# Sparse attention into a four-matrix feed-forward, one core: q and k of the local heads of batches 5 to 7 turned by DMA transposes instead of TensorE

## The chip, the core and the metric

The kernel runs on one core of a Trainium2 chip, in one launch. The metric is the device time of one execution in microseconds. Each time given is a median over several runs.

## What is computed

Eight batches, eight heads, 576 tokens, 64 values per head, all in float32. Heads 0 to 3 are *local*: a token sees itself and the 31 before it. Heads 4 to 7 are *strided*: a token sees those earlier tokens whose position is equal to its own modulo 32. What follows is a product of two linear layers and two more layers.

```python
scores = (1/sqrt(64)) * q @ k.transpose(0, 1, 3, 2)
rel = pos[:, None] - pos[None, :]
mask_local   = (rel >= 0) & (rel < 32)
mask_strided = (rel >= 0) & (pos[None, :] % 32 == pos[:, None] % 32)
attn = softmax(where(mask of the head, scores, -1e9))       # heads 0..3 local, 4..7 strided
x = (attn @ v).transpose(0, 2, 1, 3).reshape(8 * 576, 512)
out = ((x @ w1) * (x @ w2)) @ w3 @ w_out                     # w1, w2: 512x1024, w3: 1024x1024, w_out: 1024x512
```

## The kernel before, in words

**Order.** Nothing is written in its final order by hand. The kernel records operations (`plan.op`, L65) with the engines that may run them, a planned cost for each engine, dependencies, buffers taken and given, and a rank. `Plan.order` (L88) then plays them through once with those costs while the program is built, and issues every instruction in the order that comes out. Each engine works its own list strictly in that order, and an instruction that must wait holds up all that stands behind it on its engine. All DMAs, loads, stores and DMA transposes, are issued from one queue, that of SyncE (SP). Loads are taken in the order of the list `_loads` (L25).

**Feed-forward.** w3 and w_out are multiplied into one matrix `w34` at the start (transposes at L613, matmuls at L632). After that there are nine tiles of 512 tokens. Each has eight pairs of groups of four 128x512 matmuls, `a` (L902, against w1) and `b` (L918, against w2), whose product is written to `abt`, and then 32 matmuls `o` (L938) against `w34`. The attention of batch b is laid between the matmuls of tile b-1 by its ranks (`_arank`, L19).

**Attention.** Each batch is worked as four head pairs `hp`: 0 and 1 local, 2 and 3 strided. A local pair is cut into 6 blocks of 96 queries, a strided one into 8 classes of 72. For each pair: scores `S` (L751; for a local pair 12 matmuls of 96 columns with the contraction over the 64 values of a head, two heads on the two halves of the array), exp on ScalarE (L769), a mask product on VectorE (L776), `X` (L788 strided, L798 local; probabilities by values), and the normalisation. A local pair is then turned back by six transposes `U` (L867). `S` needs q and k with the head's 64 values on the partitions, so q and k have to be turned. There are two ways in the kernel:

- **On TensorE.** q and k of four heads are loaded in one go, 128 partitions of 4 tokens (`load_qk`, L490, 512 KB each), which covers 512 of the 576 tokens. The other 64 tokens of all eight heads come with `load_rest` (L506). GpSimd casts them to float16 (L310). Then `T` turns 512 tokens of q and k of one pair with eight 128x128 transposes (`fnT`, L702, matmuls at L707), two copies `E` take them from PSUM to `qT` and `kTL` or `kTS` (L717), and `R` (L652, matmuls at L657) with its copies (L665) puts in the 64 tokens left. Local pairs of all batches and strided pairs of batches 0 to 2 are done so.
- **By DMA transposes.** From batch `LB` = 3 on (`cfg lb`), strided pairs are loaded by `load_qs` (L551) as 72 partitions of 8 tokens (`load_s`, L547), cast on GpSimd into `xs16`, and turned SBUF to SBUF by a DMA transpose issued from SP (L568; its operation is `DTop`, L570). In `qT` and `kTS` the token 8w + c then lies at column 80c + w, and a class of the strided pair reads 72 columns in a row.

`qT` (L334) holds one batch. A transpose or an eviction into pair `hp` of it must wait for `S` of the same pair of the batch before; for the DMA transposes this is L571, where it is `S` of both strided pairs. Seven staging buffers `st` take the loads (L298).

The softmax here doesn't subtract the row's maximum and nothing guards it: scores larger than these inputs give would overflow.

## Time and profile before

| | |
|---|---|
| median of 8 runs | 276.09 us (275.22 to 278.59) |
| the profiled execution | 276.08 us, of which the profile's span is 274.0 us |
| instructions in the span | 6186, of them 2353 matmuls |
| busy: PE, PEld, DVE, ACT, POOL | 96%, 53%, 64%, 59%, 47% |
| granted TensorE clock | 1.00 |
| DMA | 52.56 MB, 192 GB/s on average |

PE is TensorE's matmuls and PEld its weight loads, DVE VectorE, ACT ScalarE, POOL GpSimd, SP the queue of SyncE that issues the DMAs. The matmuls are pipelined: the duration of one in the trace is longer than the distance from its start to that of the next one, and only that distance is time that a matmul costs. For example 128x512 matmuls have 379 ns each and start 216 ns apart. Durations of DMA issues are the time that SP is held by them, not the transfer.

### The profile page before, as it was taken

The page shows a single profiled execution, that of the slowest core. Times are in us where ns is not written, and L with a number is a line of the kernel's source. Part 1 is how long each engine was busy: PE and PEld are TensorE (multiplying, and loading weights), DVE is VectorE, ACT ScalarE, POOL GpSimd, SP SyncE. Part 2 cuts the span into 40 slices and gives each one's busy share as a digit, 9 for nine tenths or more (in the row PEclk, how much of TensorE's full clock was granted, in tenths as well). Part 3 has the DMA queues.
Part 4 walks back from the last instruction along what each step waited for, and adds up shares of the span by engine and source line. Part 5 has one row for each costly group of instructions (what it writes and reads, how often), then busy time and mean ns, then how long its engine had stood idle before and what let it go on. Part 6 is the DMA issues. An engine that isn't in the chain of part 4 may idle for free.

```text
span 274.0 us, 6186 instructions
## 1 busy us (share of the span) xinstructions
PE 263.5 (96%) x2353; PEld 146.0 (53%) x2353; DVE 174.6 (64%) x328; ACT 161.7 (59%) x291; POOL 128.6 (47%) x156
## 2 busy tenths in 40 slices
PE   7787899999999999999999999999999999999995
PEld 2465695746555545555555555555545544444443
DVE  6744466777677767875886788587768763321431
ACT  2871478775668745874687558755765675324321
POOL 6765997789969556586574856530000000000000
PEclk9999999999999999999999999999999999999999
DMA  7999999999999988999999999922141012003004
GB/s 255 346 352 250 321 356 364 305 262 295 321 190 204 225 185 256 279 197 168 330 264 205 229 270 233 201 92 49 28 139 41 0 41 115 0 2 153 0 0 154
DMA packets 64581, 52.56 MB, mean 192 GB/s; under 512 B 34152, under 2 KB 53864, under 8 KB 64552
## 3 DMA queue, kind: packets, MB, share of 16 engines
q1 hardware_dynamic: 64552, 52.18, 72.0%
q8 instruction: 18, 0.29, 0.5%
q14 instruction: 11, 0.09, 0.1%
HBM read 39.45 MB, written 9.44 MB: 178 GB/s over the span
## 4 chain that ended last, share of the span: by engine, by line
PE 88%; DMA 7%; POOL 1%; SPq 1%; issue 0%; DVE 0%; POOLq 0%; DVEq 0%
PE ps_o L938 23%; PE ps_b L918 23%; PE ps_a L902 23%; DMA st<-in_moe_w_dram 5%; PE ps_S L751 4%; PE ps_mm L632 3%; PE ps_X L798 3%; PE ps_T L707 3%; PE ps_X L788 3%; PE ps_U L867 2%; DMA st<-in_k_dram 2%; SPq L313 1%; POOL w3n L310 1%; PE ps_tr L613 1%; PE ps_R L657 1%; POOL v16S L310 0%
## 5 line engine op out<-in xcount | busy, mean ns | idle before, releaser
L918 PE MATMUL ps_b<-xT,w2h 128*128 128x512 f16 x288 | 73.9, 379 | 0.0
L902 PE MATMUL ps_a<-xT,w1h 128*128 128x512 f16 x288 | 73.8, 379 | 0.0
L924 DVE TENSOR_TENSOR abt<-ps_b,asb 128x512 f16<-128x512 f32 x72 | 49.4, 690 | 38.1 <-PE ps_b L918 37.7
L306 ACT COPY asb<-ps_a 128x512 f32<-128x512 f32 x72 | 42.1, 587 | 51.5 <-PE ps_a L902 51.3
L938 PE MATMUL ps_o<-w,abt 128*128 128x512 f16 (+1 forms) x296 | 67.4, 374 | 0.0
L938 PEld LDWEIGHTS <-abt 128*128 128x128 f16 x296 | 26.9, 98 | 27.7
L918 PEld LDWEIGHTS <-w2h 128*128 128x128 f16 x288 | 26.6, 98 | 28.1
L902 PEld LDWEIGHTS <-w1h 128*128 128x128 f16 x288 | 26.7, 98 | 27.7
L769 ACT ACTIVATE ps_S<-ps_S 128x576 f32<-128x576 f32 (+2 forms) x56 | 32.8, 626 | 10.5 <-PE ps_S L751 9.9
L306 ACT COPY osb<-ps_o 128x512 f32<-128x512 f32 x35 | 20.6, 588 | 20.6 <-PE ps_o L938 20.3
L310 POOL CAST v16L<-st 32x768 f16<-32x768 f32 (+1 forms) x32 | 26.3, 822 | 7.6 <-DMA st<-in_v_dram 4.6
L854 DVE TENSOR_TENSOR xT<-ps_X,rcp 64x288 f16<-64x288 f32 x56 | 25.1, 449 | 5.9 <-ACT rcp L838 5.3
L310 POOL CAST x<-st 128x1024 f16<-128x1024 f32 x22 | 22.7, 1040 | 12.2 <-DMA st<-in_q_dram 6.8
L776 DVE TENSOR_TENSOR ptm<-ps_S,maskL 128x576 f16<-128x576 f32 x28 | 19.8, 750 | 12.1 <-ACT ps_S L769 12.1
L310 POOL CAST v16S<-st 72x1024 f16<-72x1024 f32 (+1 forms) x16 | 16.5, 1037 | 13.8 <-DMA st<-in_v_dram 12.5
L310 POOL CAST xs<-st 80x1024 f16<-80x1024 f32 x20 | 20.2, 1036 | 4.7 <-DMA qT<-xs 2.6
L817 DVE TENSOR_TENSOR xqs<-ps_X,rcq 96x384 f16<-96x384 f32 (+1 forms) x36 | 20.5, 568 | 1.2
L838 ACT ACTIVATE rcp<-ps_X 64x576 f32<-64x576 f32 x28 | 18.1, 647 | 0.9
L827 ACT ACTIVATE ps_X<-ps_X 64x576 f32<-64x576 f32 x28 | 17.7, 631 | 0.9 <-PE ps_X L788 0.5
L632 PE MATMUL ps_mm<-woh,w3T 128*128 128x256 f16 x128 | 15.9, 272 | 1.6 <-POOL woh L310 1.5
L798 PEld LDWEIGHTS <-ptm 128*96 128x96 f16 (+1 forms) x224 | 14.5, 123 | 5.3
L308 DVE COPY qT<-ps_T 128x512 f16<-128x512 f16 x16 | 11.1, 692 | 7.9 <-PE ps_T L707 7.9
(81 smaller groups left out, 274.8 us busy)
## 6 DMA issues: line engine op xcount, KB each, us to landing
out_dram<-osb SPq DMA_DIRECT2D x35, 256.0 KB
st<-in_moe_w_dram SPq DMA_DIRECT2D x16, 512.0 KB
st<-in_v_dram SPq DMA_DIRECT2D x26, 288.0 KB
st<-in_q_dram SPq DMA_DIRECT2D x11, 512.0 KB
st<-in_k_dram SPq DMA_DIRECT2D x11, 512.0 KB
st<-in_q_dram SPq DMA_DIRECT2D x10, 288.0 KB
st<-in_k_dram SPq DMA_DIRECT2D x10, 288.0 KB
st<-in_moe_w_out_dram SPq DMA_DIRECT2D x4, 512.0 KB
```

What stands on the lines that cost most here:

```text
L306: pin(nc.scalar.copy(out=out, in_=in_))
L310: pin(nc.gpsimd.tensor_copy(out=out, in_=in_))
L632: pin(nc.tensor.matmul(ps, big[f"w3T{kc // 4}"][:, kc % 4, js], big["woh"][:, kc, ns], start=(kc == 0), stop=(kc == KF - 1)))
L769: pin(nc.scalar.activation(out=sps, in_=sps, func=AF.Exp, bias=0.0, scale=scale))
L776: pin(nc.vector.tensor_mul(ptm[0:kr, 0:576].rearrange("p (h a x) -> p h a x", h=2, x=w), pte[0:kr].rearrange("p h (a x) -> p h a x", x=w), ...
L798: pin(nc.tensor.matmul(xps[0:w, h, i * 65:(i + 1) * 65], ptms[pslot][0:kr, c0:c0 + w], vt[0:kr, 2 * (hp % 2) + h, g * m + i, 0:D + 1], sta ...
L817: pin(nc.vector.tensor_mul(xqs[0:w, 0:m].rearrange("p i h d -> p h i d"), xv[:, :, :, 0:D], _ap(rcp, 0, [[rcp.ap[0][0], w], [4, 2], [1, m] ...
L854: pin(nc.vector.tensor_mul(o, i0, i1))
L902: pin(nc.tensor.matmul(ps, w1h[:, ci, js], xT[ci][:, tok], start=(ci == 0), stop=(ci == KM - 1)))
L918: pin(nc.tensor.matmul(ps, w2h[:, ci, js], xT[ci][:, tok], start=(ci == 0), stop=(ci == KM - 1)))
L924: pin(nc.vector.tensor_mul(big[("abt", t)][:, jc, :], bank("f", f"b{t}_{jc}"), live[("asb", t, jc)]))
L938: pin(nc.tensor.matmul(ps, big[("abt", t)][:, ci, bass.ds(ts * P, P)], w34[:, ci, bass.ds(pt * nw, nw)], start=(ci == 0), stop=(ci == KF - ...
```

## The change

A new setting `ll=5` sends the local pairs of batches 5 to 7 through `load_qs` too. For these, `load_qk` and `load_rest` are not called, and `T`, `E`, `R` and its copies are not made (16 transposes and 8 matmuls of `R` in each of the three batches). Instead, for each local pair:

- q is loaded, cast and turned like a strided pair's: 72 rows of 8 tokens, column 80c + w for token 8w + c. A block of 96 queries is then 12 values of w by 8 of c, and `S` reads it as its moving operand with a step of 80 elements (160 bytes) between neighbouring columns.
- k is loaded in rows of single tokens (96 partitions, 12 runs of 256 bytes each, the form in which `load_vL` loads v), cast, and turned so that its tokens lie in `kTL` in their own order.

Two DMA transposes are added per local pair, 12 in all. Other parts of the diff touch all batches: `load_s` now issues two DMAs, for 64 and for 8 rows, where it issued one for 72; a DMA transpose of a pair waits for `S` of that pair of the batch before and no longer for both; the planned costs of SP and of several transfers are changed, so that the order that comes out differs in places. The settings `ub` and `nxq` are added and left at values that use none of their code.

```diff
-        r += [("qk", b, 0), ("r", b), ("vL", b, 0), ("vL", b, 1)]
-        r += [("qk", b, 1)] if b < 3 else [("qs", b, 0), ("qs", b, 1)]
+        r += [("qk", b, 0), ("r", b)] if b < 5 else [("qs", b, 0), ("qs", b, 1)]
+        r += [("vL", b, 0), ("vL", b, 1)]
+        r += [("qk", b, 1)] if b < 3 else [("qs", b, 2), ("qs", b, 3)]
...
-           first=('DVE', 'ACT', 'POOL'), early=0, pm=4, nx=4, nstg=7, new=(2, 3), lb=3)
+           first=('DVE', 'ACT', 'POOL'), early=0, pm=4, nx=4, nstg=7, new=(2, 3), lb=3, ll=5)
...
-        o = plan.op(name, {"SP": 450}, fn, take=[("stg", key)] if first else [], dma=ns)
+        o = plan.op(name, {"SP": 700 if name[:2] == "vL" else 500}, fn, take=[("stg", key)] if first else [], dma=ns)
...
-    def load_s(key, ten, b, hh):
-        src = ten[b, 4 + 2 * hh:6 + 2 * hh].rearrange("h (p c) d -> p h (c d)", c=ST)
-        return dma(key, key, 830, [P, 2, ST, D], lambda s: s[0:SQ].rearrange("p h c d -> p h (c d)"), src, clean=2)
+    def load_s(key, ten, b, hp):
+        src = ten[b, 2 * hp:2 * hp + 2].rearrange("h (p c) d -> p h (c d)", c=ST)
+        return [dma(key, key, 700, [P, 2, ST, D], lambda s: s[0:64].rearrange("p h c d -> p h (c d)"), src[0:64],
+                    clean=2),
+                dma(f"{key}b", key, 100, None, lambda s: s[64:SQ].rearrange("p h c d -> p h (c d)"), src[64:SQ],
+                    first=False)]
...
+            nat = local and nm == "k"
+            if nat:
+                ds = [dma(key, key, 1950, [P, 2, LT, D], lambda s: s[0:LQ].rearrange("p h t d -> p (h t) d"),
+                          _ap(k, (b * H + 2 * hp) * S * D, [[D, LQ], [LQ * D, 2 * LT], [1, D]]))]
+            else:
+                ds = load_s(key, ten, b, hp)
+            nr, nt = (LQ, LT) if nat else (SC, ST)
...
-                o = (qT[:, hp] if nm == "q" else kTS[:, hh, 0:ST * SC]).rearrange("x (c w) -> x c w", w=SC)
+                if nm == "q":
+                    o = qT[:, hp].rearrange("x (c w) -> x c w", w=SC)
+                elif local:
+                    o = kTL[:, hh, 32:32 + S].rearrange("x (c w) -> x c w", w=LQ)
+                else:
+                    o = kTS[:, hh, 0:ST * SC].rearrange("x (c w) -> x c w", w=SC)
...
-            late.append((o, lambda: [Sop.get((b - 1, h)) for h in (2, 3)]))
+            late.append((o, lambda: [Sop.get((b - 1, hp))]))
...
-        for i, nm in enumerate("qk"):
+        for i, nm in enumerate("qk" if b < LL else ""):
...
-            dt = b >= LB and not local
+            dt = b >= (LL if local else LB)
...
-                            pin(nc.tensor.matmul(sps[:, h, i * w:(i + 1) * w], kT[r_, ks:ks + P],
-                                                 qT[r_, hp, qs:qs + w], start=not pm, stop=not pm or i == m - 1))
+                            qq = qT[r_, hp, qs:qs + w]
+                            if dt and local:
+                                q0 = (g * m + i) * LQ // ST
+                                qq = qT[:, hp].rearrange("x (c w) -> x w c", w=SC)[r_, q0:q0 + LQ // ST]
+                            pin(nc.tensor.matmul(sps[:, h, i * w:(i + 1) * w], kT[r_, ks:ks + P], qq, start=not pm, stop=not pm or i == m - 1))
```

## The prediction

> **What bounds the kernel.** I read the page's busy rows and slices first, then its chain of waits. The columns of the second fence are the 40 slices of 6.85 us.

> ```profile
> span 274.0 us, 6186 instructions
> PE 263.5 (96%) x2353; PEld 146.0 (53%) x2353; DVE 174.6 (64%) x328; ACT 161.7 (59%) x291; POOL 128.6 (47%) x156
> ```
> ```profile
> PE   7787899999999999999999999999999999999995
> PEclk9999999999999999999999999999999999999999
> DMA  7999999999999988999999999922141012003004
> ```
> ```profile
> PE 88%; DMA 7%; POOL 1%; SPq 1%; issue 0%; DVE 0%; POOLq 0%; DVEq 0%
> ```

> PE is idle for 274.0 - 263.5 = 10.5 us, in the first five slices, where the chain runs over DMA loads of weights. From there on it is full at a granted clock of 1.00, and 88% of the chain lies on it. The list of what PE waited for, asked for 40 to 272 us alone, comes back empty. So each PE microsecond removed after 40 us is a microsecond off the end, as long as nothing becomes late. DMA is full as well until slice 26 (about 180 us) and then nearly idle; it feeds PE and does not yet hold it up.

> A busy PE is not PE at its peak, so I take prices from starts in the timeline of PE (start, duration, line):

> ```profile
> 195.40 0.43 PE L751 MATMUL ps_S<-qT,kTS 64*128 64x72 f16 x16
> 195.76 1.04 PE L938 MATMUL ps_o<-w,abt 128*128 128x512 f16 x4
> 196.64 0.40 PE L657 MATMUL ps_R<-idR,x16r 96*128 96x64 f16 x8
> 196.87 1.03 PE L938 MATMUL ps_o<-w,abt 128*128 128x512 f16 x4
> 197.74 0.42 PE L788 MATMUL ps_X<-ptm,v16S 72*128 72x72 f16 x8
> 198.00 0.61 PE L707 MATMUL ps_T<-id,x 128*128 128x128 f16 x8
> 198.45 0.42 PE L788 MATMUL ps_X<-ptm,v16S 72*128 72x72 f16 x8
> ```

> One `T` holds PE from 198.00 to 198.45, 0.45 us; one `R` from 196.64 to 196.87, 0.23 us. No idle time stands between the groups.

> **Removed from PE.** Two `T` and one `R` for each of batches 5, 6 and 7: 3 x (2 x 0.45 + 0.23) = 3.39 us, all of it on the path. The order built from the changed kernel has 72 matmuls fewer on PE, just these. Their 12 evictions `E` and 6 of `R` lie on ACT and DVE, 59% and 64% busy and on no percent of the chain: worth nothing.

> **Added on PE: a moving operand with a step.** `S` of a local pair has 12 matmuls of 96 columns, in 6 couples that run side by side on the halves of the array (starts in the trace 3 ns apart within a couple, 40 to 43 ns from one couple to the next: the 216 ns of 512 columns scaled to 96 give 40). Two pairs in three batches make 36 couples, 36 x 40 = 1.46 us of reading. Now each column of q lies 160 bytes from the last. No PE instruction before reads its moving operand so. The nearest row is a DVE copy of 128x576 float16, packed from local pairs and with a step of 8 elements from strided ones (it reads PSUM, `S` reads SBUF):

> ```profile
> L308 DVE COPY xT<-ps_U x17: 456/458/758, 18.5 to 214.8; 128x576 f16<-128x576 f16 x17
> ```

> The packed ones have 458 ns, the two with a step 756 and 758: 1.66 times. On ACT no such loss shows: 639 ns for 576 packed, 586 to 591 for 512 with a step of 4. Lower end: no loss, 0 us (there are no fewer columns to read, so no gain). Upper end: PE reads with a step no faster than that DVE row, 758/576 = 1.32 ns an element, 126 ns a couple instead of 40: 36 x 86 = 3.1 us. I take the ratio 1.66, since the row is of the same kind, two-byte elements with a step: 1.46 x 0.66 = 0.97 us.

> [...]

> **Added on SP, DMA and GpSimd, off the path if they keep up.** SP issues all DMAs in order. Its rows, in two pieces of its timeline:

> ```profile
> 64.83 2.88 SPq L313 DMA_DIRECT2D st<-in_v_dram  x4
> ...
> 77.77 0.34 SPq L313 DMA_DIRECT2D st<-in_k_dram  x1
> ```
> ```profile
> L568 SPq DMA_TRANSPOSE kTS<-xs x10: 1206/1272/2012, 95.0 to 197.6; - x10
> ```

> The first line is v of batch 2 for two strided pairs, as 64 and 8 rows each: 1.44 us per couple of DMAs. One of 72 rows has 0.34. So each strided load costs SP about 1.1 us more. Per batch from 5 on SP issues 8 such couples (11.5 us), 2 loads of k and 2 of v in rows of 256 bytes (about 0.6 each where not held up, 2.4), 8 transposes (8 x 1.27 = 10.2) and 4.5 stores (0.4 each, 1.8): 25.9 us. A batch on PE takes 26.3 us now (its first local `S` starts at 176.80 for batch 6, 203.12 for batch 7) and would take about 25.5. For batches 3 and 4 it is 6 couples, 6 packed loads and 4 transposes, about 19 us. From 75 us, where loads of batch 3 start, that makes 2 x 19 + 3 x 25.9 = 116 us of issuing, done at 191 us if SP never waits. The last transpose is needed for the last `S`, at 221.3 now and near 218.9 then, and lands 2.7 us after its issue starts (188.16 to 190.81 in the trace's completion marks): 25 us are left for waits. The first transposes of batch 7 can start when `S` of the same pair of batch 6 is through (176.8, 182.1) and are needed near 200.5. What is queued behind a waiting transpose on SP is loads of the next batch and stores; stores have three buffers on ACT's side, loads a lead of ten and more us. That cover is why I cost the 12 transposes and the split at nothing; if it is gone, the lateness goes straight to the end, since PE waits in order.

> DMA: by the completion marks, 72-row loads of 288 KB in a row land 1.6 to 1.7 us apart (81.03 to 91.09 us), two 64-row loads of 256 KB 0.6 us apart (69.58, 70.21). The split therefore saves some 0.8 us of DMA on 30 loads, about 24 us. Against it stand, for each of three batches, about 1.6 for q, 2 x 1.2 for k in rows of 256 bytes (loads of v in that form land 0.8 to 1.7 us apart) and 4 x 0.65 for transposes (175.59, 176.17, 176.91, 177.62), 6.6 in all, instead of 4.9 for the two 512 KB loads and the rest: +5 us. DMA has more room than before.

> GpSimd: two casts of 1.04 us and two of 0.61 go, two of 1.04 and two of about 0.82 come: +0.4 us a batch on an engine that is 47% busy. Nothing. The new planned costs shift PE's order between about 27 and 60 us and the strided `S` of batch 7 by one group. The work is the same; the bound is the longest single wait of PE there so far, 1.8 us for `w3n`, either way, and I take 0.

> **The sum.** Profiled execution 276.08 (span 274.0 and 2.1 around it; the median of the runs is 276.09) - 3.39 + 0.97 = 273.7 us. From the bounds of the step alone: 272.7 to 275.8. A measurement here can tell about 0.5% from no change, 1.4 us; the limits are 274.7 and 277.5.

> **Rivals.** (1) *SP becomes the clock.* In 62.5 to 200 us SP is held by its DMA issues for 94.8 us, and some 35 us of these are issues that take far longer than the same issue at its shortest (a transpose 6.2 us instead of 1.2). If these 35 us stay on top of 116 us, SP ends at 75 + 116 + 35 = 226, 10 us after the last transpose is needed, and PE stands still for them: 272.7 + 1 + 10, about 284. It decides once held-up issues and waits pass 25 us. For it: SP's sum is as long as a PE batch. Against: the long issues come where DMA is behind, and the split takes 24 us from DMA. Chance 0.16. (2) *The step costs PE two to three times the contiguous read or more*, up to the 3.1 us above: 274.7 to 276.5. For it: a step of 160 bytes is far wider than the 16 bytes of the DVE row. Chance 0.14. (3) *The freed PE time comes back as another wait*, for `ps` banks or the ACT evictions of `a`: 275 to 276. ACT waited 51.3 us for `a` and is not late, so 0.05. The forecast's own case, a step at up to 2.4 times and no late load, holds 0.65 and 272.4 to 274.7.

> **How the numbers follow.** Faster comes from the forecast's case and a little of (2): 0.67. Within 0.5%: most of (2), (3) and a mild form of (1): 0.18. Slower: the rest of (1): 0.15. The range goes from 272.4 (no loss by the step, 0.3 for the shifted order) to 276.4, which takes in (2), (3) and leaves the full (1) out, with a little beyond each end.

> **What would show it.** Right: 72 matmuls fewer, no `T` or `R` after batch 4, PE's list of waits after 40 us still empty, batches 5 to 7 shorter by 0.8 us each, and `S` of local pairs at 0.53 us from start to next group instead of 0.37. Each step can be wrong by itself: the step, if that distance is 0.37 or above 0.7; SP, if PE's weight loads of `S` wait on `qT` or `kTL`; the queue, if the last transposes land after 215 us. The forecast falls if PE shows more than a microsecond of idle time after 60 us.

## The result, and the profile after

The changed kernel takes 277.63 us (median of 11 runs, 277.31 to 279.23), the kernel before 275.78 us beside it (32 runs): the ratio is 1.0074, 95% interval 1.0055 to 1.0093. It is slower, by about 2 us, where 273.7 us and a gain of 2.4 us were forecast. The profiled execution took 277.48 us, 275.7 of them in the span: 1.7 us more span than before.

The page of the changed kernel, its first rows:

```profile
span 275.7 us, 6098 instructions
PE 266.2 (97%) x2281; PEld 144.7 (52%) x2281; DVE 170.7 (62%) x324; ACT 158.0 (57%) x277; POOL 130.6 (47%) x156
```

PE runs 72 matmuls fewer than before, just those that the forecast took off, and yet is busy for 2.7 us more. The slices, and the chain by engine and by line:

```profile
PE   8887999999999999999999999999999999999995
PEclk9999999999999999999999999999999999999999
DMA  6999999999799998799799986789969003003004
...
PE 87%; DMA 7%; SPq 2%; POOL 1%; issue 1%; ACT 1%; DVE 1%; POOLq 0%; DVEq 0%
PE ps_o L974 23%; PE ps_b L954 22%; PE ps_a L938 22%; DMA st<-in_moe_w_dram 7%; PE ps_S L776 6%; PE ps_mm L650 3%; PE ps_X L822 3%; PE ps_X L812 2%; PE ps_U L903 2%; PE ps_T L727 2%; SPq L314 2%; POOL w3n L311 1%; PE ps_tr L631 1%; PE ps_S L763 0%; PE ps_R L675 0%
```

PE is full after the first slices at the full clock, as before, and asked for 40 to 275 us the list of what PE waited for is empty again. So no wait came in: the added time is inside PE's own work. Of PE's lines on the chain one has grown, `S` (L776, L751 before): 6%, where it was 4%. Its groups, kept apart by shape, before (first line) and after:

```profile
L751 PE MATMUL ps_S<-qT,kTL 64*128 64x96 f16 x192 | 6.9, 204 | 0.0
```
```profile
L776 PE MATMUL ps_S<-qT,kTL 64*128 64x96 f16 x192 | 12.0, 264 | 0.0
```

The columns are busy us, mean ns of one, idle time before. As many matmuls of the local pairs, of one shape, are busy for 5.1 us more. All of it lies in batches 5 to 7. One local `S` group of batch 5 in the timeline of PE, before and then after; what counts is the distance from its start to that of the next group:

```profile
150.47 0.43 PE L751 MATMUL ps_S<-qT,kTL 64*128 64x96 f16 x12
150.83 1.04 PE L938 MATMUL ps_o<-w,abt 128*128 128x512 f16 x4
```
```profile
149.24 1.29 PE L776 MATMUL ps_S<-qT,kTL 64*128 64x96 f16 x12
150.46 1.04 PE L974 MATMUL ps_o<-w,abt 128*128 128x512 f16 x4
```

0.36 us became 1.22 us (0.362 and 1.220 by the trace's nanoseconds), the same in all six groups. Within a group the two matmuls of a couple still start 3 ns apart; the couples start 163 ns (the first two) to 190 ns apart, 183 ns on average, where before they started 53 ns (the first two) and 42 to 43 ns apart. The account closes: 6 x (1.220 - 0.362) = 5.15 us added, 3.41 us of `T` and `R` removed (0.451 and 0.235 a group), +1.74 us, and the span grew by 1.7.

### The profile page after: what moved, and what is told of

Read it like the earlier page. It is cut to its first block, busy times and chain, and to the rows that moved or that the text cites. A ratio compares the mean times of both kernels' runs of the same rounds, so it can differ in the third digit from the quotient of the medians.

```text
span 275.7 us, 6098 instructions
## 1 busy us (share of the span) xinstructions
PE 266.2 (97%) x2281; PEld 144.7 (52%) x2281; DVE 170.7 (62%) x324; ACT 158.0 (57%) x277; POOL 130.6 (47%) x156
## 4 chain that ended last, share of the span: by engine, by line
PE 87%; DMA 7%; SPq 2%; POOL 1%; issue 1%; ACT 1%; DVE 1%; POOLq 0%; DVEq 0%
PE ps_o L974 23%; PE ps_b L954 22%; PE ps_a L938 22%; DMA st<-in_moe_w_dram 7%; PE ps_S L776 6%; PE ps_mm L650 3%; PE ps_X L822 3%; PE ps_X L812 2%; PE ps_U L903 2%; PE ps_T L727 2%; SPq L314 2%; POOL w3n L311 1%; PE ps_tr L631 1%; PE ps_S L763 0%; PE ps_R L675 0%
## 5 line engine op out<-in xcount | busy, mean ns | idle before, releaser
L938 PE MATMUL ps_a<-xT,w1h 128*128 128x512 f16 x288 | 73.8, 379 | 0.0
L311 POOL CAST xs<-st 80x1024 f16<-80x1024 f32 (+1 forms) x32 | 31.7, 997 | 32.6 <-DMA st<-in_k_dram 19.2
L938 PEld LDWEIGHTS <-w1h 128*128 128x128 f16 x288 | 26.6, 98 | 27.6
L311 POOL CAST v16L<-st 32x768 f16<-32x768 f32 (+1 forms) x32 | 26.3, 822 | 9.1 <-DMA st<-in_v_dram 7.7
L311 POOL CAST x<-st 128x1024 f16<-128x1024 f32 x16 | 16.5, 1040 | 11.2 <-DMA st<-in_k_dram 6.9
L309 DVE COPY xT<-ps_U 128x576 f16<-128x576 f16 x17 | 8.4, 493 | 12.5 <-PE ps_U L903 12.5
```

Source lines behind the costliest of these rows:

```text
L311: pin(nc.gpsimd.tensor_copy(out=out, in_=in_))
L938: pin(nc.tensor.matmul(ps, w1h[:, ci, js], xT[ci][:, tok], start=(ci == 0), stop=(ci == KM - 1)))
```

## Experiments

All are edits of the changed kernel. A *group* is the 12 matmuls of `S` of one local pair, and its time is the distance from its start to that of the next group on PE. Times of the kernel before are from the same chip as the runs beside them. Loads, casts and DMA transposes stay as the change has them unless the edit says otherwise.

### e1: q of local pairs in single tokens, so that `S` reads columns in a row

```diff
-            nat = local and nm == "k"
+            nat = local
...
-                           _ap(k, (b * H + 2 * hp) * S * D, [[D, LQ], [LQ * D, 2 * LT], [1, D]]))]
+                           _ap(ten, (b * H + 2 * hp) * S * D, [[D, LQ], [LQ * D, 2 * LT], [1, D]]))]
...
-                if nm == "q":
+                if nm == "q" and local:
+                    o = qT[:, hp, 0:S].rearrange("x (c w) -> x c w", w=LQ)
+                elif nm == "q":
...
-                            if dt and local:
-                                q0 = (g * m + i) * LQ // ST
-                                qq = qT[:, hp].rearrange("x (c w) -> x w c", w=SC)[r_, q0:q0 + LQ // ST]
```

> The changed kernel, but q of the local pairs of batches 5 to 7 is loaded in rows of single tokens like k and lies in qT in its own order, so that S reads 96 columns in a row; all else, the 12 DMA transposes too, stays. Theory A (the step of 160 bytes in the moving operand is the loss: the trace of the changed kernel shows a local S group at 1.22 us to the next group instead of 0.36): these groups go back to 0.36 us, PE loses 6 x 0.86 = 5.15 us, and the span is about 275.7 - 5.15 = 270.6 us, some 1.2% below the kernel before. Rival B (the loss comes from what feeds S: the transposed k in kTL, the fuller SP queue, later landings): the groups stay near 1.2 us and the time within 0.5% of the changed kernel, 276 to 279 us. Rival C (q in rows of 256 bytes makes DMA late): S groups at 0.36 us but PE waits between groups, 272 to 276 us.

280.47 us (278.76 to 280.55) against 275.88; ratio 1.0147, interval 1.0115 to 1.018. The local `S` groups are back at 0.361 us, so the stepped read made them long. But the time rose. PE's waits from 57 us on, and the slices, of this run:

```profile
PE ps_S L775 <- DVE xT L882: 1.7, 2, 0.9
PE ps_a L937 <- DVE xT L882: 1.2, 1, 1.2
PE ps_X L811 <- DVE ptm L799: 1.1, 2, 0.7
...
PE   7787999999999999999999999999999958999995
PEclk9999999999999999999999999999999995999999
```

At 224 to 231 us PE stands five times, for the attention of batch 7 alone: the DVE steps of one pair's attention no longer lie beside other PE work. From the third stop on its clock is down (the 5 at 229 to 236 us) and the 128x512 matmuls start 0.42 to 0.43 us apart instead of 0.216. Added up by starts the stops make about 5 us and the slow clock about 2, a little more than the 277.1 - 270.6 = 6.5 us of span above the expectation. This is the trace of an execution of 278.77 us; four of the six took 280.45 to 280.55, and no trace shows what these 1.7 us more are. No transpose was late: the last `kTS` landed at 215.95, and the `S` that follows on it ran at 225.26. Its place in PE's order was late. This kernel plans its q loads of local pairs at 1950 ns where the change has 700 and 100, so the planner put `S` of batch 7's pairs later. That is a reading; e1b tests it.

### e2: the rest of the change alone

```diff
-        r += [("qk", b, 0), ("r", b)] if b < 5 else [("qs", b, 0), ("qs", b, 1)]
+        r += [("qk", b, 0), ("r", b)] if b < 8 else [("qs", b, 0), ("qs", b, 1)]
...
-           first=('DVE', 'ACT', 'POOL'), early=0, pm=4, nx=4, nstg=7, new=(2, 3), lb=3, ll=5)
+           first=('DVE', 'ACT', 'POOL'), early=0, pm=4, nx=4, nstg=7, new=(2, 3), lb=3, ll=8)
```

> The changed kernel with ll=8: no local pair is turned by DMA, T and R are as before in all batches. What is left of the change is the split of the 72-row loads into 64 and 8 rows, the transposes' wait for one S instead of two, and the new planned costs with the order that comes of them. Theory A: this rest is worth nothing to PE, ratio to the kernel before 0.997 to 1.003. Rival B (the rest is a part of the loss): slower by 0.5% or more. If the rest is a gain hidden by the step: faster by 0.5% or more.

276.23 us (275.34 to 278.88) against 275.88; ratio 1.0012, interval 0.9989 to 1.0035. Split loads, planned costs and the looser wait together are worth nothing that can be told: no loss, and no gain either. The loss is that of the local pairs.

### e3: six steps in one run

Each of the six local `S` groups reads as many columns as before, 96, with another step. They are other columns than the scores need, so the output is not that of the reference.

```diff
-                                qq = qT[:, hp].rearrange("x (c w) -> x w c", w=SC)[r_, q0:q0 + LQ // ST]
+                                st_ = (2, 4, 8, 16, 32, 64)[2 * (b - LL) + hp]
+                                qb = qT[r_, hp, 0:ST * SC]
+                                qq = _ap(qb, q0, [[qb.ap[0][0], 64], [1, 12], [st_, 8]])
```

> The changed kernel, where each local pair of batches 5, 6 and 7 reads q with another step, so that S reads wrong columns of q there (the scores of these pairs are not the reference's); as before 12 groups of 8 columns. Steps in order of the pairs: 2, 4, 8, 16, 32, 64 elements of 2 bytes. Theory A1 (a new 16-byte piece of SBUF at each column is what costs): steps 2 and 4 near 0.36 us for a group of 12 matmuls, steps 8 to 64 all at about 1.2 us. Theory A2 (any step but 1 costs the same): all six at about 1.2 us. Theory A3 (the loss grows with the distance): a rise from step to step, 64 highest.

There is one execution, with a span of 273.8 us, and one group for each step; in the change all six groups took the same 1.22 us, so a difference between groups here is one of the step. The timeline of PE for steps of 2, 4, 8, 32 and 64 elements, each group and the start of the next:

```profile
149.15 0.47 PE L778 MATMUL ps_S<-qT,kTL 64*128 64x96 f16 x12
149.55 0.82 PE L976 MATMUL ps_o<-w,abt 128*128 128x512 f16 x3
...
154.49 0.75 PE L778 MATMUL ps_S<-qT,kTL 64*128 64x96 f16 x12
155.17 0.30 PE L905 MATMUL ps_U<-id,xqs 96*128 96x96 f16 x3
...
174.70 1.17 PE L778 MATMUL ps_S<-qT,kTL 64*128 64x96 f16 x12
175.80 0.39 PE L976 MATMUL ps_o<-w,abt 128*128 128x512 f16 x1
...
201.42 1.14 PE L778 MATMUL ps_S<-qT,kTL 64*128 64x96 f16 x12
202.49 0.39 PE L976 MATMUL ps_o<-w,abt 128*128 128x512 f16 x1
...
207.43 1.14 PE L778 MATMUL ps_S<-qT,kTL 64*128 64x96 f16 x12
208.51 0.39 PE L905 MATMUL ps_U<-id,xqs 96*128 96x96 f16 x5
```

0.40, 0.68, 1.10, 1.08 and 1.08 us (and 1.14 for 16). The price grows up to a step of 8 elements, 16 bytes, and not beyond; the change's own 80 elements cost a little more, 1.22. That a step of 4 would be near 0.36 was wrong: it already costs 0.32 us more.

With a step of 4, most 16-byte pieces of `qT` give two columns in a row, and the group takes 0.68 us all the same: two columns to a piece did not bring PE back to 0.36.

### e4: runs of neighbouring columns

The six groups read runs of 2, of 4, of 8 and of 12 columns, then a mixture in which the upper half of the array steps by 80 elements and the lower reads in a row, then 96 in a row. Again they are other columns than the scores need.

```diff
+                                off, pat = ((0, [[2, 6], [80, 8], [1, 2]]), (0, [[4, 3], [80, 8], [1, 4]]),
+                                            (0, [[40, 12], [1, 8]]), (q0, [[80, 8], [1, 12]]),
+                                            (q0, [[1, 12], [80, 8]] if h == 0 else [[1, 96]]),
+                                            (q0, [[1, 96]]))[2 * (b - LL) + hp]
+                                qq = _ap(qb, off, [[qb.ap[0][0], 64], *pat])
```

> The changed kernel, where each local pair of batches 5 to 7 reads q in another pattern of 96 columns (the scores of these pairs are not the reference's): runs of 2 columns in a row, each run 160 bytes from the last; runs of 4; runs of 8, 80 bytes apart, at 16-byte boundaries; runs of 12, 160 bytes apart; a step of 160 bytes in the upper half of each couple and 96 in a row in the lower half; and 96 in a row in both. If the cost goes by jumps (Theory A1), with about 1.5 us of extra time per 1000 jumps as in the changed kernel (147 ns for a couple's 96): runs of 2 give a group of 0.36 + 0.43 = 0.8 us, of 4 about 0.57, of 8 and 12 about 0.43 to 0.46, or none if a run hides its jump. The half-and-half pattern gives 1.2 us if the halves wait for each other, and the last one 0.36 us. Rival B (k or the DMA feeding): all near 1.2 us.

One execution. The timeline of PE for runs of 2, of 4 and of 8, and for the mixture:

```profile
150.89 0.73 PE L781 MATMUL ps_S<-qT,kTL 64*128 64x96 f16 x12
151.55 0.39 PE L979 MATMUL ps_o<-w,abt 128*128 128x512 f16 x1
...
156.49 0.46 PE L781 MATMUL ps_S<-qT,kTL 64*128 64x96 f16 x12
156.88 0.43 PE L908 MATMUL ps_U<-id,xqs 96*128 96x96 f16 x6
...
176.42 0.43 PE L781 MATMUL ps_S<-qT,kTL 64*128 64x96 f16 x12
176.78 1.04 PE L979 MATMUL ps_o<-w,abt 128*128 128x512 f16 x4
...
201.61 1.28 PE L781 MATMUL ps_S<-qT,kTL 64*128 64x96 f16 x12
202.83 0.39 PE L979 MATMUL ps_o<-w,abt 128*128 128x512 f16 x1
```

0.66, 0.39, 0.36 us, 0.36 for runs of 12, 1.22 for the mixture and 0.36 for 96 in a row. A fixed price for each jump had called for 0.8, 0.57 and 0.43 to 0.46, so that is not the rule. Jumps cost nothing here once eight columns follow on each other (80 bytes from run to run) or twelve (160 bytes), 0.36 us as for 96 in a row. With one half stepping the group takes as long as with both, 1.22 us: the slower half set its time.

### e5: the change with runs of 12

For one and the same data in `qT`, `S` reads c outside and w inside: 8 runs of 12 columns. The queries of a block then come in another order, which a permuted mask and the copy from `U` to `xT` put right (which then reads with a step: 0.76 us on DVE instead of 0.46, and planned at 760 ns instead of 450).

```diff
-                                qq = qT[:, hp].rearrange("x (c w) -> x w c", w=SC)[r_, q0:q0 + LQ // ST]
+                                qq = qT[:, hp].rearrange("x (c w) -> x c w", w=SC)[r_, :, q0:q0 + LQ // ST]
...
-            kr, mk = (P, maskL) if local else (SQ, maskK) if dt else (KB, maskS)
+            kr, mk = (P, maskP if dt else maskL) if local else (SQ, maskK) if dt else (KB, maskS)
...
+                if local and dt:
+                    copy(e, o.rearrange("x (t w c) -> x t w c", w=LQ // ST, c=ST),
+                         ps[:, 0:S].rearrange("x (t c w) -> x t w c", w=LQ // ST, c=ST))
```

> The changed kernel, loads and DMA transposes untouched, but S of the local pairs of batches 5 to 7 reads its 96 columns as 8 runs of 12 in a row instead of one column at each 160-byte step; the queries of a block then stand in another order, so these pairs get a permuted mask, and the copy from U to xT puts the order right again (VectorE 0.30 us more for each of 6 copies, beside the path). Theory A (the jumps at each column are the whole loss): the S groups at 0.36 us as in the run with runs of 12, span 275.7 - 5.15 = 270.6 us, ratio to the kernel before 0.985 to 0.991. Rival (with PE faster, the transposes from SP become late, as the last one landed 10 us before its S in the changed kernel): idle time on PE near 215 to 230 us, 273 to 277 us.

274.87 us (273.5 to 276.66) against 275.93; ratio 0.9953, interval 0.9929 to 0.9978: faster than before, with the loads and transposes of the change as they were, but short of the expected 0.985 to 0.991. The span, 272.3, is 1.7 above what was expected, and PE's waits from 57 us on show most of it:

```profile
PE ps_S L780 <- DVE xT L887: 0.8, 1, 0.8
PE ps_a L945 <- DVE xT L887: 0.4, 1, 0.4
```

`S` of batch 7's first pair stands at 200.72 us, half through, for `xT` of the attention before it; both `kTL` of the batch had landed by 196.44. So it is not a transfer. In e1b, below, 16 matmuls `o` stand between the last `X` before this `S` and the `S`, here 8, and the normalisation has less time: it reads as the planned order again, but no run tests that here.

### e1b: e1 with its loads planned short

```diff
-                ds = [dma(key, key, 1950, [P, 2, LT, D], lambda s: s[0:LQ].rearrange("p h t d -> p (h t) d"),
+                ds = [dma(key, key, 1200, [P, 2, LT, D], lambda s: s[0:LQ].rearrange("p h t d -> p (h t) d"),
```

(on top of e1, so it counts for q and k of these pairs; the number is used by the planner alone)

> The run with q in rows of single tokens again, but with 1200 instead of 1950 as the planned DMA cost of such a load. In that run S was back at 0.36 us and yet the time was longer, since the planned order set attention of batch 7 behind most of tile 6, and its last normalisation stood bare before tile 7. With the shorter cost the order that comes out sets S of batch 7 at the places that it has in the kernel before. If only the planned order was at fault: about 272 to 273 us, ratio 0.985 to 0.992. If the loads or transposes of batch 7 are late in fact: PE waits at S of batch 6 or 7, 274 to 281 us.

272.14 us (272.07 to 272.45) against 275.93; ratio 0.9854, interval 0.982 to 0.9889. This is the best of all the versions. From its page:

```profile
span 270.6 us, 6088 instructions
PE 260.4 (96%) x2281; PEld 142.4 (53%) x2281; DVE 170.7 (63%) x324; ACT 157.6 (58%) x277; POOL 129.2 (48%) x156
```

The span is 274.0 - 3.4 = 270.6: all of `T` and `R` gained, nothing given back. The list of waits from 57 us on is empty, the local `S` groups take 0.361 us, and the last `kTS` lands at 207.40, 10.6 us ahead of the `S` that needs it (218.02; the pair before it has its `S` at 210.72, with `kTS` since 206.15). `S` of batch 7's pairs start at 199.87 to 218.02, 5 to 8 us earlier than in e1. One planned number made the difference between e1 and e1b: 6.5 us between the two profiled spans, 8.3 us between the medians.

### e5 and e1b with another first batch

```diff
-           first=('DVE', 'ACT', 'POOL'), early=0, pm=4, nx=4, nstg=7, new=(2, 3), lb=3, ll=5)
+           first=('DVE', 'ACT', 'POOL'), early=0, pm=4, nx=4, nstg=7, new=(2, 3), lb=3, ll=6)
```

> Runs of 12 as in its neighbour, but for batches 6 and 7 alone (ll=6): two thirds of the removed T and R, 2.27 us instead of 3.41. Theory A: 1.1 us slower than the one from batch 5, ratio to the kernel before 0.989 to 0.995. If SP holds up the one from batch 5, this one is the faster of the two.

> Runs of 12 for batches 4 to 7 (ll=4): T and R of four batches gone, 4.55 us. The planned order sets attention of batch 7 behind most of tile 6, as in the run with q in rows. If PE alone counts: 1.1 us faster than from batch 5, ratio 0.981 to 0.987. If SP is the clock at four batches with 20 DMAs and 8 transposes each: the end of batch 7 stands bare, slower than from batch 5 by 2 us or more.

> Edit: e1b (q of local pairs in rows of single tokens, its load planned at 1200) with the change from batch 4 on instead of batch 5. If PE alone counts: 1.13 us less than e1b (two T of 0.45, one R of 0.23), span 269.5, 271.0 us, ratio to the kernel before 0.981 to 0.983. Rival: with a fourth batch through SP and the DMA transposes the attention of batch 7 is set or fed late, as in the runs-of-12 version from batch 4: idle PE at 200 to 232 us and 274 us or more. It decides whether batch 5 was the right place to begin.

e5 from batch 6: 274.7 us, ratio 0.9941 (0.992 to 0.9962), the same as from batch 5 within the intervals; one batch less to gain from, and fewer stops. e5 from batch 4: 281.43 us, ratio 1.0182 (1.0144 to 1.0219). e1b from batch 4: 276.63 us, ratio 1.0019 (0.9995 to 1.0042), 4.5 us more than from batch 5, where PE's work alone would have given 1.1 less. PE's waits from 57 us on in e5 from batch 4:

```profile
PE ps_a L945 <- DVE xT L887: 4.4, 3, 2.2
PE ps_X L816 <- DVE ptm L804: 1.8, 2, 1.5
```

Again the attention of batch 7 comes late and its DVE steps lie bare (in e1b from batch 4 from 225 to 230 us; the granted clock of that execution is 0.987 on the mean of its span, where e1b has 1.00), though the last `kTS` had landed at 216.65 and 217.64 and the last `S` ran at 226.81 and 224.37. What of this is the planned order and what a late transpose of an earlier pair was not separated.

### e6: is it the run, or the 16 bytes?

Steps of 2 cost as much as runs of 4 (0.40 and 0.39 us), steps of 4 as much as runs of 2 (0.68 and 0.66). That fits a price for each 16-byte block that PE goes on to. The first three of the six patterns here move the runs off the blocks; the others go between two places, go round four, and step by 6. Again they are other columns than the scores need.

```diff
+                                off, pat = ((4, [[40, 12], [1, 8]]), (6, [[16, 3], [80, 8], [1, 4]]),
+                                            (7, [[8, 6], [80, 8], [1, 2]]), (0, [[1, 48], [80, 2]]),
+                                            (0, [[1, 24], [80, 4]]),
+                                            (0, [[1, 12], [6, 8]]))[2 * (b - LL) + hp]
```

> Edit: as e4, with six other reading patterns of q in the six local S groups of batches 5 to 7; these groups read the wrong columns, 96 as ever. In order: runs of 8 that begin at element 4 of a block of 8 (a block is 16 bytes); runs of 4 that begin at element 6; runs of 2 that begin at element 7; columns alternating between two places 80 elements apart; columns going round four places 80 elements apart; step 6. Theory L (what counts is how often PE has to go on to another 16-byte block, about 1.45 to 1.95 ns each by the groups measured so far, with the contiguous 40 ns a couple as floor): the patterns change block 24, 48, 96, 96, 96 and 74 times, so the groups take 0.36 to 0.40, 0.66 to 0.68, 1.08 to 1.22, 1.08 to 1.22, 1.08 to 1.22 and about 0.85 to 0.95 us. Rival R (the length of the run counts, wherever it lies): 0.36, 0.39, 0.66 as measured for aligned runs of 8, 4 and 2, and 1.08 to 1.22 for the other three. Rival H (several blocks are held, so that coming back to one is free): the fourth and fifth at 0.36 to 0.40. Span near 270.6 plus what the six groups take above 0.362 each.

One execution. The timeline of PE for the second, third and fourth pattern (runs of 4 and of 2 across a block's edge, two places in turn):

```profile
155.48 0.74 PE L781 MATMUL ps_S<-qT,kTL 64*128 64x96 f16 x12
156.15 0.43 PE L908 MATMUL ps_U<-id,xqs 96*128 96x96 f16 x6
...
175.68 1.28 PE L781 MATMUL ps_S<-qT,kTL 64*128 64x96 f16 x12
176.90 0.39 PE L979 MATMUL ps_o<-w,abt 128*128 128x512 f16 x1
...
181.83 0.72 PE L781 MATMUL ps_S<-qT,kTL 64*128 64x96 f16 x12
182.49 0.30 PE L908 MATMUL ps_U<-id,xqs 96*128 96x96 f16 x3
```

Runs of 4 take 0.67 us when they straddle an edge and 0.39 when they do not; runs of 2 take 1.21 and 0.66. The length of the run does not explain that, the number of blocks does (48 and 24, 96 and 48). The first, fifth and sixth pattern fit too (0.365, 1.083 and 0.904 us). The fourth does not: two places in turn take 0.655 us, where a new block at each column should give 1.08 or more; four places in turn (1.083) are at the full price. So going back to the block of two columns before cost less than going on to a new one, and going back to that of four columns before cost as much; why stays open.

## Why the prediction was wrong, step by step

**What bounds the kernel** held: PE is full after 57 us before and after, at the full clock, and where no wait came in PE's time moved the end one for one (after +1.74 for +1.7 of span, e1b -3.4 for -3.4).

**The removal from PE** held: 3.39 forecast, 3.41 by the starts, 72 matmuls, and e1b shows it whole at the end.

**The step that failed is the price of the moving operand with a step**: 0.97 us taken, 3.1 us as the upper end, 5.15 us measured. 0.858 us a group is 143 ns a couple, from 40 to 183, 4.6 times; 27 were taken and 86 were the bound. The prediction's sign that a distance above 0.7 us would show this step wrong came out at 1.22. Three errors lie in it. The ratio 1.66 came from a DVE copy, whose contiguous read is itself slow (458 ns for 576 elements, 0.8 ns each); PE starts from 0.42 ns a column, so even the same loss for each element, 0.52 ns, would have been a ratio of 2.2. The bound took for granted that PE reads with a step no slower than DVE; nothing in the trace of before said so. PE took 183 / 96 = 1.91 ns a column, DVE 1.32 ns an element. And the rows were misread: in the kernel before, that copy (L880) reads PSUM with a step of 72 elements, 144 bytes, not 8, and ACT's copy (L721) with one of 128, not 4. ACT showed no loss and DVE 1.66 at steps nearly as wide as the 160 bytes of `S` or wider; the two engines differed, which was a reason to trust neither for PE. With 5.15 in the forecast's own sum, 276.08 - 3.39 + 5.15 = 277.84, against 277.48 in the profiled execution.

**SP, DMA and GpSimd at nothing** held for this change: e2 and e1b show it, and no transpose was late. The last two `kTL` and the last `kTS` in the timeline of SP, after:

```profile
191.99 1.22 SPq L586 DMA_TRANSPOSE kTL<-xs  x1
...
194.62 1.31 SPq L586 DMA_TRANSPOSE kTL<-xs  x1
...
210.89 1.24 SPq L586 DMA_TRANSPOSE kTS<-xs  x1
```

They land at 196.29, 197.47 and 214.28, and their `S` start at 203.07, 209.22 and 224.66. The bound of 215 us was kept by a hair: the 191 us of issuing without waits became 212, so 21 of the 25 us kept for waits were used.

The estimate of DMA behind this term was wrong all the same. It had 24 us saved by the split and 5 us added, "more room than before". The time that the packets of the DMA queue took (packets, MB, share of 16 engines' span), before, with the rest of the change alone (e2), and after:

```profile
q1 hardware_dynamic: 64552, 52.18, 72.0%
```
```profile
q1 hardware_dynamic: 64912, 52.18, 70.1%
```
```profile
q1 hardware_dynamic: 76576, 53.66, 78.1%
```

Of spans of 274.0, 274.7 and 275.7 us that is 197, 193 and 215 us: the split took off some 5 us, and the local pairs' loads and transposes put on some 23 beyond what they replace. DMA got fuller by 18 us instead of emptier by 19, and it cost nothing only because PE waited for none of it.

**The shifted order at 0** held here and is the weakest point beyond: e1 lost 6.5 us of span to the planner's order, and e5 1.7, which is read the same way. **Rival 2** named the right mechanism and capped it too low, at 3.1 us. Its reason, that 160 bytes are far wider than the DVE row's 16, does not stand: that row's step is 144 bytes, and e3 has PE at almost the whole price from 16 bytes on. **Rival 1** did not happen. What resembles it, the versions from batch 4, stood for late attention, and there a late transpose of an earlier pair was not ruled out.

## What to carry to other kernels

In these groups of 96 columns of float16, runs of 8 and of 12 columns cost what 96 in a row cost (0.36 us), runs of 4 took 0.39 us within 16-byte blocks and 0.67 across their edges, runs of 2 took 0.66 and 1.21, and steps of 8 elements and more 1.08 to 1.22. So count the blocks that a matmul's pattern goes through, and choose the layout of the load or the transpose so that the matmul reads in a row (e1b), or reorder the loops of the pattern (e5), before giving up the cheaper path. An upper bound taken from another engine is no bound (1.32 ns an element on DVE, 1.91 ns a column on PE); when a row for the engine itself is missing, keep the range open on that side. And where a planner writes the order, a changed cost figure is a change of the program: e1 and e1b differ in one such number and by 8.3 us in their medians.
